# Row side of a gated linear attention: two-source copies of a, products, a guard and a copy on GpSimd, and stash copies in runs of four

## The chip, the cores and the metric

One NeuronCore of a Trainium2 chip runs the whole program. The metric is the device time of one execution, in microseconds (us). The engines are PE (TensorE, matrix products and transposes), DVE (VectorE), ACT (ScalarE), POOL (GpSimd), and SP (SyncE), whose queue issues most of the DMAs.

## The reference

Three layers follow one another. The first, which this change is about, is a linear attention whose state decays by a complex gate:

```python
scale = np.minimum(mag, 0.999) / (mag + 1e-06)      # mag = |a|
a_re_n, a_im_n = (a_re * scale, a_im * scale)
for t in range(S):                                  # S = 768
    new_re = ar * S_re - ai * S_im
    new_im = ar * S_im + ai * S_re
    S_re, S_im = (new_re + kv, new_im)              # kv: outer product of k and v
    y[:, :, t] = einsum('bhd,bhde->bhe', q[:, :, t], S_re)
```

Batch 4, 8 heads, head size 48. Behind it come a mixture of 8 experts on the tokens with a positive skip score, and a dense layer with a leaky activation (384 to 2048 to 384). All arrays are float32.

## The kernel before, in words

The batch is cut into two halves (`ui` 0 and 1), and the sequence into 8 chunks of 96 steps. A "row" is one chunk of one head of one sequence; a half has 128 rows, one per partition. Within a chunk the state is replaced by running products P of the gates: q is multiplied by P and k is divided by it, after which a chunk is matrix products. The row side (`attention_rows`, line 154) computes P, q times P and k over P for all 128 rows; the chunk side (`attention_chunks`, line 495) uses them. Both are done for half 0, then the experts and the dense layer of half 0 run woven with the row side of half 1, and so on.

The row side of half 0 works on blocks of steps (`BLKA`: one of 4 steps, ten of 8, then 6, 4 and 2). For each block there are these pieces:
- `load_a`, `load_kq` (lines 199, 205): DMAs on SP's queue. The tile of a has 3 buffers and that of k and q has 2, so `load_a(i + 3)` stands behind the last reader of block i's tile, in `norm` (line 251).
- `norm_pre` (211): on ACT squares, logarithm, exponential, square and the *guard* s2, a scale and an offset of r0. The sum of the two squares is a product with the identity on PE (tile `ad`, in PSUM), for blocks 0 to 2 a sum on DVE.
- `norm` (233): three steps on DVE into `nrr`, the third of which reads the guard; then the products of a with the scale, into columns 0 and 2 of the tile `a4`; then two copies into columns 3 and 1 of it, plain and negated (lines 255 to 261). Blocks 0 and 1 make these copies on DVE, others on ACT, and 11 to 13 the plain one on POOL (lists `MIRROR`, `MIRROR_G`; the guard of blocks 10, 11 and 13 is on POOL by `GUARD_G`).
- `steps` (335): the running product, one step after the other: a product of 192 elements into `t`, and a sum of 96 elements into P. The very first step is a copy of a into P (line 341).
- `scaled_pre`, `scaled` (263, 277): the norm of P on ACT and PE gives `pg`; on DVE two products of q with P (tile `qr`), two steps into `pu` (the first reads `ad` in PSUM and `pg`), a product into k, and two products of k with P (tile `kr`).
- `turned` (315): transposes on PE of four steps of `kr` or `qr` at a time into PSUM, and a copy by ACT into the *stash* (line 324), the layout the chunk side reads: partition = part and feature, then chunk, row and step.

In the same time `gate_products` (451) puts products of v with the gate weights on PE and ACT (tiles `gv`, `gvT`, `gps`).

Which instruction comes when is written by hand for half 0: `timed` (372) gives each piece a time in a plan (a block of n steps is 2n long, `AT_NORM`, `AT_SCALED` and so on are shares of it), and the instructions are issued in that order. DVE, ACT and PE keep it strictly (`keep("VAT")`); the order on POOL is left to the framework's scheduler, which takes what is ready, first what was written first. Every queue then runs in order. Before the row side is issued, the two stash tiles have their last 32 partitions zeroed on POOL:

```python
    gen = attention_rows(0, ep, BLKA, True, nc.sync, rws[0], stash, more)
    next(gen)
    constants()
...
    for x in stash:
        G.memset(x[2 * D:].rearrange("p c b t -> p (c b t)"), 0.0)
    run(gen)
```

The trace puts nearly all compute under line 91, the helper that records an instruction, so its rows are told apart by tile names.

Of the kernel before, what the change touches and what calls it, by code (L numbers as in the profile page):

```python
# [14 lines left out]
ALU = mybir.AluOpType  # L15
# [4 lines left out]
B, H, S, D = 4, 8, 768, 48  # L20
# [46 lines left out]
SUM_NORM = (0, 1, 2)  # L67
SUM_SCALED = (12, 13)
MIRROR = (0, 1)
GUARD_G = (10, 11, 13)  # L70
MIRROR_G = (11, 12, 13)
LISTS = dict(sp=(0, 1), tp=(2, 3, 7), yps=(4,), ups=(5,), tr=(6,), bk=(7,))
DEEP = {"kqt": 3, "vt": 3, "qT": 3}
LISTSA = dict(sp=(0, 1), yps=(2,), ups=(3,), tr=(4, 5, 6), bk=(7,))
# [4 lines left out]
def moe_attention_kernel(ctx, tc, q, k, v, a_re, a_im, w_skip, w_gate, w1, w2, w_in, w_out, out,  # L79
# [15 lines left out]
    V, A, T, G = Engine(nc.vector, "V"), Engine(nc.scalar, "A"), Engine(nc.tensor, "T"), Engine(nc.gpsimd, "G")  # L95
# [58 lines left out]
    def attention_rows(ui, ep, blks, sum_pe, queue, store, stash=None, more=None):  # L154
# [9 lines left out]
        nb = len(blks)  # L164
        tbm = max(blks)

        def rows(src, i):
            return src[b0:b0 + HB].rearrange("b h (c t) d -> c (b h) (t d)", t=L)[
                :, :, t0s[i] * D:(t0s[i] + blks[i]) * D]

        def flat(x):
            return x.rearrange("p t d -> p (t d)")

        def cost(i, n=1):
            return (70 + 1.04 * n * blks[i] * D) / 1e3

        def tl(tag, i, dims=(), after=(), bufs=None):
            kw = {} if bufs is None else {"bufs": bufs}
            t = ep.tile([R, *dims, tbm, *after, D], F32, tag=tag, name=tag, **kw)
            n = blks[i]  # L180
            return t[:, :, :n] if len(dims) == 1 else t[:, :n]

        def both(x, i):
            return x.unsqueeze(2).to_broadcast([R, blks[i], 2, D])

        a4s, Ps, ins, pre, turns, lags = {}, {}, {}, {}, [], []
# [12 lines left out]
        def load_a(i):  # L199
            ari = tl("ari", i, (2,), bufs=3)  # L200
            queue.dma_start(flat(ari[:, 0]), rows(a_re, i))
            queue.dma_start(flat(ari[:, 1]), rows(a_im, i))
            ins["a", i] = ari

        def load_kq(i):
            kq2 = tl("kq2", i, (2,))
            queue.dma_start(flat(kq2[:, 0]), rows(k, i))
            queue.dma_start(flat(kq2[:, 1]), rows(q, i))
            ins["k", i] = kq2

        def norm_pre(i):
# [14 lines left out]
            A.activation(rr, r0, AF.Square)  # L226
            if stash and i in GUARD_G:
                G.tensor_scalar(s2, r0, 0.5e-6 / MAGCAP, -0.5, ALU.mult, ALU.add)
# [4 lines left out]
        def norm(i):  # L233
            ari = ins.pop(("a", i))
            m2, s2, r0, rr = pre["a", i]
            V.tensor_tensor(rr, m2, rr, ALU.mult)
            yield cost(i)
            V.scalar_tensor_tensor(rr, rr, 3.0, r0, ALU.subtract, ALU.mult)
            yield cost(i)
            V.scalar_tensor_tensor(rr, rr, -2.0, s2, ALU.max, ALU.mult)  # L240
            yield cost(i)
            a4 = tl("a4", i, (), (4,))
            a4s[i] = a4
            if stash:
                V.tensor_tensor(a4[:, :, 0, :], ari[:, 0], rr, ALU.mult)
                yield cost(i)
                V.tensor_tensor(a4[:, :, 2, :], ari[:, 1], rr, ALU.mult)
            else:
                V.tensor_tensor(a4[:, :, 0::2, :], ari.rearrange("p c t d -> p t c d"), both(rr, i), ALU.mult)
            if i + 3 < nb:  # L250
                load_a(i + 3)
            yield cost(i, 2)
            for _ in range(3 if ui else 0):
                yield 0.0
            for c in range(2):
                if stash and i in MIRROR_G and not c:
                    G.tensor_scalar(a4[:, :, 3 - 2 * c, :], a4[:, :, 2 * c, :], 1.0 - 2 * c, None, ALU.mult)
                elif stash and i in MIRROR:
                    V.tensor_scalar(a4[:, :, 3 - 2 * c, :], a4[:, :, 2 * c, :], 1.0 - 2 * c, None, ALU.mult)
                else:  # L260
                    A.activation(a4[:, :, 3 - 2 * c, :], a4[:, :, 2 * c, :], AF.Copy, scale=1.0 - 2 * c)

        def scaled_pre(i):
            P = Ps[i]
            sq = ep.tile([R, tbm, 2, D], F32, tag="psq", name="psq")[:, :blks[i]]
            g0 = tl("pg0", i)
            A.activation(sq, P, AF.Square)
            yield
            n2 = added(sq[:, :, 0, :], sq[:, :, 1, :], i, SUM_SCALED)
            yield  # L270
            s2 = sq[:, :, 1, :]
            A.activation(s2, n2, AF.Ln)
            yield
            A.activation(g0, s2, AF.Exp, scale=-1.0)
            pre["k", i] = n2, g0

        def scaled(i):
            P = Ps.pop(i)
            kq2 = ins.pop(("k", i))
            u = tl("pu", i)  # L280
            if stash:
                kq = [tl(x, i, (), (2,)) for x in ("kr", "qr")]
            else:
                kq = tl("kq", i, (), (2, 2))
                kq = [kq[:, :, a] for a in range(2)] + [kq]
            if stash:
                V.tensor_tensor(kq[1][:, :, 0], kq2[:, 1], P[:, :, 0], ALU.mult)
                yield cost(i)
                V.tensor_tensor(kq[1][:, :, 1], kq2[:, 1], P[:, :, 1], ALU.mult)
            else:  # L290
                V.tensor_tensor(kq[1], both(kq2[:, 1], i), P, ALU.mult)
            yield cost(i, 2)
            n2, g0 = pre["k", i]
            V.tensor_tensor(u, n2, g0, ALU.mult)
            yield cost(i)
            V.scalar_tensor_tensor(u, u, 2.0, g0, ALU.subtract, ALU.mult)
            yield cost(i)
            V.scalar_tensor_tensor(kq2[:, 0], kq2[:, 0], -1.0, u, ALU.mult, ALU.mult)
            yield cost(i)
            if stash:  # L300
                V.tensor_tensor(kq[0][:, :, 0], kq2[:, 0], P[:, :, 0], ALU.mult)
                yield cost(i)
                V.tensor_tensor(kq[0][:, :, 1], kq2[:, 0], P[:, :, 1], ALU.mult)
            else:
                V.tensor_tensor(kq[0], both(kq2[:, 0], i), P, ALU.mult)
            if i + 2 < nb:
                load_kq(i + 2)
            if stash:
                turns.append(turned(i, kq))
            else:  # L310
                queue.dma_start(kqd[t0s[i]:t0s[i] + blks[i]].rearrange("t r a d -> r t (a d)"),
                                kq[2].rearrange("r t a c d -> r t (a c d)"))
            yield cost(i, 2)

        def turned(i, kq):

            for g in range(0, blks[i], 4):
                m = min(4, blks[i] - g)
                for a in range(2):
                    p = ps.tile([2 * D, m, R], F32, tag="qk", name="qkps")  # L320
                    for j in range(m):
                        T.transpose(p[:, j, :], kq[a][:, g + j].rearrange("p c d -> p (c d)"), ident)
                    t = t0s[i] + g
                    lags.append((stash[a][:2 * D, :, :, t:t + m].rearrange("p c b t -> p t (c b)"), p))
                    if len(lags) > 1:
                        A.activation(*lags.pop(0), AF.Copy)
                    yield
# [7 lines left out]
        def steps(i, prev):  # L335
            a4 = a4s.pop(i)
            P = ep.tile([R, tbm, 2, D], F32, tag="P", name="P", bufs=3)[:, :blks[i]]
            Ps[i] = P
            for t in range(blks[i]):
                if prev is None:  # L340
                    V.tensor_copy(P[:, t], a4[:, t, 0::2, :])
                else:
                    t4 = ep.tile([R, 2, 2, D], F32, tag="t4", name="t4", bufs=3)
                    V.tensor_tensor(t4, prev.unsqueeze(1).to_broadcast([R, 2, 2, D]),
                                    a4[:, t].rearrange("p (o i) d -> p o i d", i=2), ALU.mult)
                    yield 0.33
                    V.tensor_tensor(P[:, t], t4[:, :, 0, :], t4[:, :, 1, :], ALU.add)
                prev = P[:, t]
                yield 0.23
# [830 lines left out]
    stash = [p.tile([128, NCH, HB * H, L], F32, name="stash") for p in blocks]  # L1180
    ep = tc.alloc_tile_pool(name="rows0", bufs=2, side="right")
    more = []
# [3 lines that stand above are left out]
# [12 lines left out]
    rt = tc.alloc_tile_pool(name="rt", bufs=1, side="right")  # L1198
    ck[0].take(1)
    behind = attention_rows(1, ep, BLKB, False, nc.sync, rws[1])  # L1200

    def place(e, layer):
# [237 lines left out]
```

## Time and profile before

| | |
|---|---|
| median of 3 runs | 968.27 us (965.54 to 970.45) |
| the profiled execution's own time | 965.6 us |
| its span | 963.3 us |
| PE, DVE, ACT, POOL busy | 87%, 65%, 54%, 14% of the span |

The span runs from the first to the last instruction of the profiled execution; its own time is 2.3 us longer. Rows of the timeline give start, length, engine, line, operation, the written tile and what it reads, the shape, and in brackets the idle time before it with what ended it. "x2" is two instructions that follow each other, merged into one row. Instructions of an engine overlap a little, so the next can start before the last one's end.

### The profile page before, as it was taken

What the parts mean: (1) busy time and instruction counts of PE and PEld (TensorE: products, weight loads), DVE (VectorE), ACT (ScalarE), POOL (GpSimd) and SP (SyncE); (2) the same over time, 40 slices, a digit from 0 to 9 for tenths busy, and PEclk for the clock granted to TensorE, in tenths of its full rate; (3) what the DMA queues carried; (4) which work ended last, traced back from release to release, by engine and by line L of the source; (5) the groups of instructions that cost most, each with busy time, mean ns of one, the idle gap of its engine ahead of it and who ended that gap; (6) DMA issues with size and microseconds to landing.
All of it is one profiled execution on the core that took longest, in us unless ns stands there. A gap on an engine that the chain in (4) does not pass through costs nothing.

```text
span 963.3 us, 17827 instructions
## 1 busy us (share of the span) xinstructions
PE 835.0 (87%) x6674; PEld 581.0 (60%) x6674; DVE 628.5 (65%) x1534; ACT 517.9 (54%) x1065; POOL 137.2 (14%) x168
## 2 busy tenths in 40 slices
PE   0488877899569975699999988999999999999997
PEld 0366666899458853344556978945677645546454
DVE  7998796477868678999990456487668262260440
ACT  2578898566445443564751777656557162250430
POOL 9100011212163001100002211141101000000000
PEclk9978798999879988799999999999999999999999
DMA  4265552798848985625436799332857201000000
GB/s 113 70 184 149 149 143 87 201 264 268 272 152 280 318 289 181 222 86 177 145 97 174 196 256 246 107 119 100 266 182 246 79 9 51 17 0 26 9 10 27
DMA packets 126512, 143.61 MB, mean 149 GB/s; under 512 B 34058, under 2 KB 109514, under 8 KB 126416
## 3 DMA queue, kind: packets, MB, share of 16 engines
q1 hardware_dynamic: 106064, 107.88, 38.2%
q10 hardware_dynamic: 18304, 29.89, 9.6%
q0 software_dynamic: 2048, 4.61, 1.4%
q8 instruction: 54, 0.88, 0.4%
q14 instruction: 42, 0.34, 0.1%
HBM read 115.62 MB, written 28.41 MB: 150 GB/s over the span
## 4 chain that ended last, share of the span: by engine, by line
PE 52%; DVE 19%; DMA 15%; ACT 10%; issue 3%; SPq 1%; POOL 0%; ACTq 0%; DVEq 0%; POOLq 0%
PE ops L91 17%; PE hps L91 13%; PE yps L91 7%; PE sps L91 3%; DVE gg L91 3%; DMA raw<-in_moe_w_in_dram 3%; DVE gl L91 3%; DVE cst L91 3%; ACT stash L91 2%; DVE a L91 2%; ACT gh L91 2%; DMA kqt<-kqd 2%; PE tps L91 2%; PE ad L91 2%; DMA vt<-vd 2%
## 5 line engine op out<-in xcount | busy, mean ns | idle before, releaser
L91 PE MATMUL hps<-xTh,m2w 128*128 128x512 f16 x576 | 173.7, 381 | 0.4 <-ACT xTh L91 0.2
L91 PEld LDWEIGHTS <-m2w 128*128 128x128 f16 x864 | 84.4, 98 | 100.3 <-issue 3.2
L91 PE MATMUL ops<-m2w,gh 128*128 128x384 f16 x512 | 125.2, 326 | 0.0
L91 PE MATMUL hps<-xTl,m2w 128*128 128x512 f16 x288 | 109.3, 380 | 0.2 <-DVE xTl L91 0.2
L91 DVE TENSOR_TENSOR gg<-hps,gg 128x512 f32<-128x512 f32 x96 | 65.8, 686 | 65.1 <-ACT gg L91 64.7
L91 PE MATMUL ops<-m2w,gl 128*128 128x384 f16 x256 | 83.6, 327 | 0.0
L91 ACT ACTIVATE ot<-ops 128x384 f32<-128x384 f32 x24 | 11.6, 489 | 121.3 <-PE ops L91 121.3
L91 PEld LDWEIGHTS <-gh 128*128 128x128 f16 x512 | 50.1, 98 | 32.7
L91 DVE TENSOR_TENSOR t<-P,a 128x192 f32<-128x192 f32 x190 | 67.1, 353 | 1.3 <-ACT a L91 0.4
L91 PE MATMUL ops<-m2w,stash 128*128 128x384 f16 x384 | 65.3, 326 | 1.2 <-ACT m2w L91 1.2
L91 DVE TENSOR_TENSOR gl<-gg,gh 128x512 f16<-128x512 f32 x64 | 44.2, 690 | 33.9 <-ACT gh L91 33.2
L91 ACT ACTIVATE gg<-hps 128x512 f32<-128x512 f32 x96 | 56.3, 587 | 17.4 <-PE hps L91 12.0
L91 DVE SCALAR_TENSOR_TENSOR w<-cw,w 128x768 f16<-128x768 f32 x64 | 59.8, 953 | 7.3 <-ACT w L91 7.1
L91 ACT ACTIVATE gh<-gg 128x512 f16<-128x512 f32 x64 | 40.3, 630 | 42.9 <-DVE gg L91 42.7
L91 ACT ACTIVATE w<-cw 128x768 f16<-128x768 f32 x64 | 53.0, 843 | 18.1 <-DMA cw<-in_moe_w_dram 15.7
L91 POOL TENSOR_SCALAR_AFFINE_SELECT sc<-sc 96x384 f32<-96x384 f32 x64 | 35.2, 559 | 156.2 <-ACT sc L91 156.0
L91 PE MATMUL ad<-psq,ident 128*128 128x384 f32 (+2 forms) x48 | 24.9, 657 | 36.8 <-ACT psq L91 36.2
L91 PEld LDWEIGHTS <-stash 128*128 128x128 f16 x384 | 37.5, 98 | 28.6 <-issue 4.3
L91 POOL DMA_INDIRECT xd<-xo,idx x16 | 25.2, 1575 | 179.6 <-DVE xo L91 165.8
L91 ACT ACTIVATE stash<-qkps 96x512 f32<-96x512 f32 (+1 forms) x50 | 50.1, 1026 | 0.3 <-PE qkps L91 0.3
L91 DVE TENSOR_TENSOR P<-t 128x96 f32<-128x96 f32 x190 | 48.1, 253 | 1.6
L91 PE MATMUL yps<-stash,hh 128*128 128x384 f32 x128 | 44.7, 503 | 3.5 <-ACT hh L91 3.5
(245 smaller groups left out, 1786.1 us busy)
## 6 DMA issues: line engine op xcount, KB each, us to landing
stash<-in_moe_w_dram ACTq DMA_DIRECT2D x32, 768.0 KB
cw<-in_moe_w_dram SPq DMA_DIRECT2D x64, 384.0 KB
kqt<-kqd SPq DMA_DIRECT2D x16, 576.0 KB
kqd<-kq SPq DMA_DIRECT2D x14, 576.0 KB
vd<-gv SPq DMA_DIRECT2D x32, 192.0 KB
vt<-vd SPq DMA_DIRECT2D x32, 192.0 KB
raw<-in_moe_w_in_dram SPq DMA_DIRECT2D x16, 384.0 KB
raw<-in_moe_w_out_dram SPq DMA_DIRECT2D x16, 384.0 KB
```

The source lines that it names most:

```text
L91: ins = getattr(self.engine, op)(*args, **kw)
```

## The change

The plain copies of a that DVE makes in blocks 0 and 1 read the load and the scale again (two sources) in place of column 0 or 2 of `a4`, so the next load into that tile stands behind them. The first step of P is the maximum of a with itself. The guard of every block from 1 on, the plain copy of every block from 2 on and both products with q of blocks 0 to 10 are on POOL. The stash copy writes, for each feature, four steps in a row, and reads PSUM across the transposes.

```diff
-GUARD_G = (10, 11, 13)
-MIRROR_G = (11, 12, 13)
+GUARD_G = range(1, 14)
+MIRROR_G = range(2, 14)
+SCALED_G = range(11)
@@ norm
-            if i + 3 < nb:
+            if i + 3 < nb and not (stash and i in MIRROR):
                 load_a(i + 3)
...
                 elif stash and i in MIRROR:
-                    V.tensor_scalar(a4[:, :, 3 - 2 * c, :], a4[:, :, 2 * c, :], 1.0 - 2 * c, None, ALU.mult)
+                    V.scalar_tensor_tensor(a4[:, :, 3 - 2 * c, :], ari[:, c], 1.0 - 2 * c, rr, ALU.mult, ALU.mult)
                 else:
                     A.activation(a4[:, :, 3 - 2 * c, :], a4[:, :, 2 * c, :], AF.Copy, scale=1.0 - 2 * c)
+            if i + 3 < nb and stash and i in MIRROR:
+                load_a(i + 3)
@@ scaled
             if stash:
-                V.tensor_tensor(kq[1][:, :, 0], kq2[:, 1], P[:, :, 0], ALU.mult)
+                X = G if i in SCALED_G else V
+                X.tensor_tensor(kq[1][:, :, 0], kq2[:, 1], P[:, :, 0], ALU.mult)
                 yield cost(i)
-                V.tensor_tensor(kq[1][:, :, 1], kq2[:, 1], P[:, :, 1], ALU.mult)
+                X.tensor_tensor(kq[1][:, :, 1], kq2[:, 1], P[:, :, 1], ALU.mult)
@@ turned
-                    lags.append((stash[a][:2 * D, :, :, t:t + m].rearrange("p c b t -> p t (c b)"), p))
+                    lags.append((stash[a][:2 * D, :, :, t:t + m].rearrange("p c b t -> p (c b) t"),
+                                 p.rearrange("p t r -> p r t")))
@@ steps
-                    V.tensor_copy(P[:, t], a4[:, t, 0::2, :])
+                    V.tensor_tensor(P[:, t], a4[:, t, 0::2, :], a4[:, t, 0::2, :], ALU.max)
```

## Rows read from the trace of the kernel before

**Rows 1.** The page: busy time, share of the span and instructions of each engine.

```profile
PE 835.0 (87%) x6674; PEld 581.0 (60%) x6674; DVE 628.5 (65%) x1534; ACT 517.9 (54%) x1065; POOL 137.2 (14%) x168
```

**Rows 2.** Busy us by stretch: PE, PEld, DVE, ACT, POOL; clock, DMA share, GB/s.

```profile
60.00:70.00 10.00, 8.30 (x40) 5.95 (x40) 7.83 (x24) 6.84 (x14) 0.00 (x0) 0.66 0.63 161
...
120.00:130.00 10.00, 7.64 (x62) 6.01 (x61) 9.70 (x30) 9.62 (x20) 0.85 (x1) 1.00 0.57 146
...
146.00:164.00 18.00, 11.89 (x85) 9.14 (x84) 13.23 (x48) 17.10 (x37) 4.78 (x7) 0.87 0.29 86
```

**Rows 3.** Timeline of the start, 0 to 32 us, all engines.

```profile
0.96 0.15 POOL L91 MEMSET w<- 112x72 f32 x1
...
1.26 0.28 POOL masks.py:199 TENSOR_SCALAR_AFFINE_SELECT ident<-ident 128x128 f32<-128x128 f32 x1
...
6.35 20.73 POOL L91 MEMSET stash<- 32x12288 f32 x2
...
8.62 0.62 DVE L91 TENSOR_TENSOR a<-ari,nrr 128x192 f32<-128x192 f32 x2
...
9.16 18.04 DVE L91 TENSOR_SCALAR a<-a 128x192 f32<-128x192 f32 x2
...
10.28 0.51 ACT L91 ACTIVATE nsq<-nr 128x384 f32<-128x384 f32 x1
...
14.98 0.62 SPq L201 DMA_DIRECT2D ari<-in_a_re_dram  x1
...
28.56 0.55 DVE L91 SCALAR_TENSOR_TENSOR nrr<-nrr,nsq 128x384 f32<-128x384 f32 x1
...
30.75 0.60 SPq L201 DMA_DIRECT2D ari<-in_a_re_dram  x1
...
30.87 0.62 DVE L91 TENSOR_SCALAR a<-a 128x384 f32<-128x384 f32 x2
```

**Rows 4.** Timeline of DVE, 40 to 160 us: pu in five blocks, a q product.

```profile
47.35 0.55 DVE L91 TENSOR_TENSOR pu<-ad,pg 128x384 f32<-128x384 f32 x1
...
126.03 0.56 DVE L91 TENSOR_TENSOR pu<-ad,pg 128x384 f32<-128x384 f32 x1 [0.16 <-ACT pg L91]
...
135.94 0.56 DVE L91 TENSOR_TENSOR pu<-ad,pg 128x384 f32<-128x384 f32 x1 [0.48 <-ACT pg L91]
...
141.81 0.55 DVE L91 TENSOR_TENSOR qr<-kq,P 128x384 f32<-128x384 f32 x1
142.28 0.35 DVE L91 TENSOR_TENSOR t<-P,a 128x192 f32<-128x192 f32 x1
...
145.36 0.56 DVE L91 TENSOR_TENSOR pu<-ad,pg 128x384 f32<-128x384 f32 x1 [1.67 <-ACT pg L91]
...
152.71 0.46 DVE L91 TENSOR_TENSOR pu<-ad,pg 128x288 f32<-128x288 f32 x1 [1.21 <-ACT pg L91]
```

**Rows 5.** Waits, 36 to 165 us: who waited for whom, total, times, longest.

```profile
DVE pu L91 <- ACT pg L91: 13.7, 11, 2.8
```

**Rows 6.** Groups by shape, 0 to 180 us (the last: instructions of tile LG).

```profile
L91 ACT ACTIVATE stash<-qkps 96x512 f32<-96x512 f32 x46 | 48.0, 1063 | 0.0
...
L91 ACT ACTIVATE a<-a 128x384 f32<-128x384 f32 x18 | 8.4, 513 | 0.3 <-DVE a L91 0.2
...
L91 ACT ACTIVATE sT<-stp 96x512 f32<-96x512 f32 x2 | 1.2, 594 | 2.0 <-PE stp L91 1.9
...
L91 DVE TENSOR_REDUCE LG<-xps x32: 217/229/232, 177.8 to 629.1; 96x9 f32<-96x72 f32 x32
```

**Rows 7.** Timeline, 117 to 145 us: one-source operations of POOL, and a DVE product.

```profile
119.24 0.51 POOL L91 TENSOR_SCALAR nsq<-nr 128x384 f32<-128x384 f32 x1 [92.16 <-ACT nr L91]
...
132.16 1.25 POOL L91 TENSOR_SCALAR a<-a 128x288 f32<-128x288 f32 x1 [2.26 <-DVE a L91]
...
141.27 2.55 POOL L91 TENSOR_SCALAR a<-a 128x192 f32<-128x192 f32 x1 [7.86 <-DVE a L91]
...
132.53 0.58 DVE L91 TENSOR_TENSOR t<-P,a 128x192 f32<-128x192 f32 x1
```

## The prediction

> **What bounds it now.** I read the page first: over the whole span PE is the busiest engine [rows 1], but that is a mean, and the change touches one stage (but for one copy), the row side of the first half, which ends at 164 us. So the next view is the busy time by stretch. In 120 to 130 us DVE and ACT are both about 96% busy with PE's granted clock at 1.00; in 60 to 70 us PE is busy 8.30 of 10 us on two thirds of the matmuls at a clock of 0.66 (mostly its lower level, 1.2 GHz), and DVE idles; in 146 to 164 us ACT alone is full [rows 2]. All three take their instructions in a written order, so the one that is late holds the others.
>
> The timeline of the start shows the largest hole: DVE's two copies of a take 18.04 us, where such a tile's products ended in 0.62 us for two. They lie beside GpSimd's two memsets of the stash and end with them [rows 3]. During the same memset the two-source products on DVE ran at their usual length [rows 3]: a one-source copy is held by it, a two-source operation isn't.
>
> From there the pace is read at one DVE operation per block, the product into pu. From block 1 (47.35 us) to block 10 (145.36 us) are 9 periods, mean 98.01 / 9 = 10.89 us; the period from 126.03 to 135.94 us is 9.91 us, and there DVE hardly waits [rows 4]. The view of waits gives what the others lose: before pu DVE waited 11 times for ACT, 13.7 us [rows 5]. So ACT sets the long periods (directly, or by leaving PE idle, behind which its clock falls), and DVE the short ones.
>
> **Part 1, the two-source copies.** The block 0 copies and the first copy into P become two-source operations and, by the row of the products during the memset, aren't held: some 0.3 us each, done by 9.9 us. That would free 17 us. But the guard list now begins at block 1, and that guard is on GpSimd, whose queue has both memsets ahead of it: its input is there at 10.3 us, where ACT computed it before in 0.51 us, and the queue is free at 27.08 us [rows 3]. Behind it on DVE wait the third step of block 1's norm and, in order, everything else; ACT's next norm step waits for a sum of DVE there. With 0.51 us for the guard [rows 7] and 0.06 us for the release, that third step starts at 27.65 us instead of 28.56: 0.9 us gained, not 17. Block 1's two copies now run one element a cycle, 2 x 0.47 = 0.94 us instead of 0.62: 0.3 us back. **Start: -0.6 us.** The two loads of a that move behind the copies: block 3's comes to SP's queue after the loads of v anyway, at 14.98 us; block 4's (30.75 us) moves by about 0.3 us, with the next loads of v and k behind it on SP's queue. Its tile is wanted some 10 us later, so I cost it at nothing; without that cover it would be 0.3 us. The second half's row side also has the copy into P, once; a few hundredths of a us, under other work.
>
> The Trainium skill (SBUF — State Buffer, Who interferes with whom) says that a VectorE operation with two SBUF inputs contends with a GpSimd one that reads SBUF, not with one that only writes. The rows of the memset agree. It gives nothing for the in-order queue, on which my -0.6 us hangs.
>
> **Part 2, per block 2 to 10.** DVE loses two q products of 0.47 us each (0.55 long, the next starts 0.47 after) [rows 4]: -0.94 us. ACT loses a guard (0.51) and a copy (0.51 [rows 6]), in its overlapped stream 0.9 us together. GpSimd gets four operations that read SBUF. Its copy of 384 elements takes 0.51 us when alone; beside a dense DVE one of 192 elements took 2.55 us, and one of 288 elements 1.25 us while DVE's t went from 0.35 to 0.58 us [rows 7]. So they exclude each other, and DVE wins more often. What one costs in port time I take from the memset, 10.4 us / 12288 = 0.85 ns an element: 0.33 us for 384 (for 288 elements 0.24, near the 0.23 that t lost). A two-source product is not in the trace on GpSimd; bounds are 0.51 us (one source) and 2.55 us (starved); I take two passes, 0.65 us of port and 0.84 us in all, since nothing else differs from the nearest row, the 0.51. Sum per block: 2 x 0.33 + 2 x 0.65 = 1.96 us. DVE has two products per block with a PSUM operand (into nrr and pu), 2 x 0.47 = 0.94 us, under which GpSimd can read; 1.02 us remains. A DVE-bound block becomes 9.91 - 0.94 + 1.02 = **9.99 us**; with all of GpSimd's reads hidden 8.97, with none 10.93.
>
> The Trainium skill (GPSIMD Engine Reference, Engine selection) advises against two-input work on GpSimd, about twice as slow. From its 4497 ns for 2048 elements an estimate is 0.84 us for 384, and the sum would not change.
>
> Results come late but have room: a q product is wanted some 8 us after its issue, a guard or copy some 5 us. GpSimd has only these in its queue after 28 us.
>
> **Part 3, the stash copies.** Each writes 512 elements one stash row apart and takes 1063 ns; the copy of the same shape from PSUM that writes a dense row takes 594 [rows 6]. Runs of four should come near the latter. In exchange its PSUM source is read with a stride. DVE's reduction of 72 strided PSUM elements takes 229 ns [rows 6], about its fixed cost, so I expect no loss there; on ACT no row shows it. Bounds: 594 ns, or no better than 1063 (a loss isn't excluded). I take 594, -0.47 us each, 4 per block: with the 0.9 above ACT has 2.8 us less of about 9.5 per block. It is then no bound, PE has fewer idle spells, and the mean period should fall to DVE's: (10.89 - 9.99) x 9 = **-8.1 us** (bounds -17.3 and +0.4).
>
> From 146 to 164 us ACT is busy 17.10 of 18 us and DVE 13.23 [rows 2], waiting for ACT (1.21 us before block 11's pu [rows 4]). The dozen full copies there give back 12 x 0.47 = 5.6 us, DVE's idle 4.8 us is the most that can show; some of it is DVE's own dependences, so **-3 us** (bounds 0 and -4.8).
>
> **Sum.** 0.6 + 8.1 + 3 = 11.7 us; later stages begin that much sooner and are not touched. Against the profiled execution's own 965.6 us that is 953.9; it lies 2.7 us under the median of the three runs, so at the median 968.3 - 11.7 = **956.6 us**. Its own range is 945 to 966 by the bounds.
>
> **Rivals.**
> A, the start comes free. The order on GpSimd isn't always that of the code: the mask of ident ran at 1.26 us, behind a memset written later [rows 3]. If block 1's guard stands ahead of the memsets, or its wait is not as I read it, steps begin at about 11.3 instead of 27.65 us: 16.3 us more, 940.3. Against it: that swap was over a short wait, and both memsets are ready first.
>
> B, slower: GpSimd holds DVE out. Place: blocks 2 to 10. If each of its operations shuts DVE out for its full length (2 x 0.51 + 2 x 0.84 = 2.70 us, none of it under a product with a PSUM operand) and DVE waits 0.57 us for the guard besides, a block takes 9.91 - 0.94 + 2.70 + 0.57 = 12.24 us: +1.35 x 9 = 12.2, less 3.6 for start and tail, 976.9. It decides from a period of 10.89 us on. For it: the 2.55 us copy; against it: DVE's stretched t is the only one of that size. The Trainium skill (SBUF — State Buffer, Who interferes with whom) says that the second to issue blocks fully until the first ends. By that rule B is the outcome where GpSimd issues first; the trace has DVE winning mostly.
>
> C, the stash copies don't get faster, the strided PSUM read costing what the strided write did. Then ACT loses only 0.9 us a block, half of the middle's gain stays, none of the tail's: 0.6 + 4 = 4.6 us, 963.7.
>
> **Numbers.** My forecast 0.60, A 0.10, B 0.14, C 0.16. A measurement of this kernel tells a change from none at about 0.5%, 4.8 us. Faster: 0.55 of the forecast, A, and half of C, 0.72; same: 0.05, the rest of C and 0.04 of B, 0.18; slower: 0.10. From 940 to 969 lie the forecast, C and half of A; outside are some 0.17.
>
> **What would show it.** Right: GpSimd's first guard at 27 us with DVE waiting for it; copies into P before 10 us; stash copies near 0.6 us; pu to pu near 10 us with few waits for pg. Wrong: DVE running steps at 12 us (A); pu periods over 10.9 us, DVE's t well over 0.35 us, waits for GpSimd (B); stash copies at 1 us or more (C); DVE waiting for loads of a or kq, now wanted sooner.

## The result, and the profile after

The changed kernel runs in 961.05 us (median of 7 runs, 956.0 to 962.5) against 970.19 us before (median of 7): ratio 0.9914, 95% interval 0.9887 to 0.9942, or 8.3 us faster (5.6 to 11.0). The profiled execution took 961.61 us, with a span of 959.9. The forecast was 956.6 us, 11.7 us less than before. Four marks of the row side show where the time went; "first kps" is the chunk side's first transpose, which needs the whole stash.

| mark (start, us) | before | after | gained in the stretch |
|---|---|---|---|
| third norm step of block 1 | 28.56 | 27.56 | 1.00 |
| pu of block 1 | 47.35 | 48.35 | -2.00 |
| pu of block 10 | 145.36 | 141.61 | 4.75 |
| first kps | 164.11 | 157.27 | 3.09 |
| sum | | | 6.84 |

What follows the row side took 799.2 us of the one span and 802.6 of the other; over all the kernels below it took 798.4 to 806.3 us. So single profiles don't show the total to better than some 4 us, and the stretches are read instead.

The timeline of the start of the changed kernel (helper line 92 now):

```profile
6.32 20.61 POOL L92 MEMSET stash<- 32x12288 f32 x2
...
9.28 0.62 DVE L92 SCALAR_TENSOR_TENSOR a<-ari,nrr 128x192 f32<-128x192 f32 x2
9.81 0.25 DVE L92 TENSOR_TENSOR P<-a 128x96 f32<-128x96 f32 x1
...
27.02 0.51 POOL L92 TENSOR_SCALAR nsq<-nr 128x384 f32<-128x384 f32 x1
27.56 0.56 DVE L92 SCALAR_TENSOR_TENSOR nrr<-nrr,nsq 128x384 f32<-128x384 f32 x1 [15.62 <-POOL nsq L92]
```

The copies of a take 0.62 us beside the memset, where they took 18.04 [rows 3]: the two sources do what was said of them. Behind them and the first copy into P, DVE runs three more operations and stops. The bracket of the last row names the cause: 15.62 us for the guard on POOL, which starts when the memsets end.

Its groups by shape, 0 to 180 us, and one block in the timeline, DVE's rows first, then POOL's:

```profile
L92 DVE TENSOR_TENSOR t<-P,a 128x192 f32<-128x192 f32 x95 | 37.8, 397 | 0.8
L92 DVE TENSOR_TENSOR P<-t 128x96 f32<-128x96 f32 x95 | 29.0, 305 | 1.4
...
L92 ACT ACTIVATE stash<-qkps 96x512 f32<-96x512 f32 x46 | 26.5, 584 | 0.2
L92 POOL TENSOR_TENSOR qr<-kq,P 128x384 f32<-128x384 f32 x20 | 23.2, 1182 | 25.8 <-DVE P L92 23.4 <-PE gtps L92 2.5
...
L92 POOL TENSOR_SCALAR a<-a 128x384 f32<-128x384 f32 x9 | 13.7, 1522 | 21.3 <-DVE P L92 14.1 <-DVE a L92 7.2
```

```profile
101.39 0.55 DVE L92 TENSOR_TENSOR pu<-ad,pg 128x384 f32<-128x384 f32 x1
...
105.34 0.60 DVE L92 TENSOR_TENSOR P<-t 128x96 f32<-128x96 f32 x1
105.86 1.36 DVE L92 SCALAR_TENSOR_TENSOR nrr<-nrr,nr 128x384 f32<-128x384 f32 x1
...
109.08 0.55 DVE L92 TENSOR_TENSOR a<-ari,nrr 128x384 f32<-128x384 f32 x1
109.55 0.66 DVE L92 TENSOR_TENSOR t<-P,a 128x192 f32<-128x192 f32 x1
...
111.78 0.55 DVE L92 TENSOR_TENSOR pu<-ad,pg 128x384 f32<-128x384 f32 x1
...
104.46 2.35 POOL L92 TENSOR_TENSOR qr<-kq,P 128x384 f32<-128x384 f32 x2 [2.61 <-DVE P L92]
109.15 1.50 POOL L92 TENSOR_SCALAR a<-a 128x384 f32<-128x384 f32 x1 [2.35 <-DVE P L92]
111.64 0.59 POOL L92 TENSOR_SCALAR nsq<-nr 128x384 f32<-128x384 f32 x1 [0.99 <-POOL a L92]
```

The stash copy fell from 1063 to 584 ns. On DVE three rows of the block are too long, and each lies beside a POOL row: P 0.60 for 0.25 and nrr 1.36 for 0.55 beside the two q products (1.16 us in all), t 0.66 for 0.35 beside the copy of a (0.31 us). (The shorter lengths are those of the same rows in E3 below, where GpSimd has no work there.) The guard at 111.64 us falls under pu, whose operand is in PSUM, and costs nothing. The block takes 10.39 us, and DVE is busy without a gap. Its waits for ACT (27 to 165 us) are nearly gone, 1.5 for 13.7 us [rows 5], and the long one at the start stands in the same view:

```profile
DVE nrr L92 <- POOL nsq L92: 15.6, 1, 15.6
...
DVE pu L92 <- ACT pg L92: 1.5, 2, 1.0
```

### The profile page after: what moved, and what is told of

Same layout as the page of the kernel before. It is cut to its first block, busy times and chain, and to the rows that moved or that the text cites. A ratio compares the mean times of both kernels' runs of the same rounds, so it can differ in the third digit from the quotient of the medians.

```text
span 959.9 us, 17852 instructions
## 1 busy us (share of the span) xinstructions
PE 832.1 (87%) x6674; PEld 580.4 (60%) x6674; DVE 618.9 (64%) x1512; ACT 493.4 (51%) x1046; POOL 178.1 (19%) x209
## 4 chain that ended last, share of the span: by engine, by line
PE 53%; DVE 23%; DMA 12%; ACT 5%; issue 4%; POOL 2%; SPq 1%; ACTq 0%; DVEq 0%; POOLq 0%
PE ops L92 17%; PE hps L92 13%; PE yps L92 7%; PE sps L92 4%; DVE gg L92 3%; DMA raw<-in_moe_w_in_dram 3%; DVE t L92 2%; DVE cst L92 2%; DVE gl L92 2%; ACT gh L92 2%; PE tps L92 2%; PE ups L92 2%; DVE P L92 2%; DVE nrr L92 2%; DMA kqt<-kqd 2%
## 5 line engine op out<-in xcount | busy, mean ns | idle before, releaser
L92 DVE TENSOR_TENSOR t<-P,a 128x192 f32<-128x192 f32 x190 | 71.1, 374 | 1.6 <-ACT a L92 0.6
L92 DVE TENSOR_TENSOR P<-t 128x96 f32<-128x96 f32 x190 | 53.0, 279 | 1.9
L92 PE MATMUL ad<-psq,ident 128*128 128x384 f32 (+2 forms) x48 | 22.7, 609 | 33.6 <-ACT psq L92 33.5
L92 ACT ACTIVATE hh<-hps 128x256 f32<-128x256 f32 (+1 forms) x64 | 23.7, 377 | 41.1 <-PE hps L92 35.9
```

Of the source, the lines that this page charges most:

```text
L92: ins = getattr(self.engine, op)(*args, **kw)
```

## The experiments

Times are medians, ratios are to the kernel before, with their intervals. "Period" is the mean of the nine from block 1's pu to block 10's: 10.89 us before, 10.36 after.

**E1, block 1's guard back on ACT.**

```diff
-GUARD_G = range(1, 14)
+GUARD_G = range(2, 14)
```

> Block 1's guard back on ACT, all else as changed. Queue theory (the hole at the start is now block 1's guard behind the memsets in GpSimd's queue): DVE's third norm step of block 1 starts near 11.7 us instead of 27.56, and DVE stops about 7 us of work later, at block 2's third norm step, whose guard is now the first one behind the memsets, until 27.5 us. So about 7 us less than the changed kernel: 954 us. Rival (the first loads set the start): DVE waits for loads, not for GpSimd, and the time stays within 2 us of the changed kernel's.

954.7 us, ratio 0.9826 (0.9782 to 0.9870). The timeline:

```profile
27.02 0.51 POOL L92 TENSOR_SCALAR nsq<-nr 128x384 f32<-128x384 f32 x1
27.56 0.56 DVE L92 SCALAR_TENSOR_TENSOR nrr<-nrr,nsq 128x384 f32<-128x384 f32 x1 [9.82 <-POOL nsq L92]
```

The rows look like those of the changed kernel, but it is block 2's guard now, and the wait is 9.82 us for 15.62. Block 1's pu starts at 42.16 us, 6.19 earlier than in the changed kernel, near the 7 expected.

**E2, the guards of blocks 1 and 2 back on ACT.** The list is `range(3, 14)`.

> The guards of blocks 1 and 2 back on ACT. Queue theory: no DVE step before 27 us needs GpSimd any more (block 3's guard is wanted near 28 us), so steps run from 10 us on and the row side ends some 14 to 15 us sooner than in the changed kernel: 946 to 947 us. Rival (first loads): less than 5 us sooner.

950.3 us, ratio 0.9781 (0.9737 to 0.9825). Block 1's pu starts at 36.77 us, 11.58 earlier than in the changed kernel, not 14 to 15. The timeline says what is left:

```profile
27.02 1.19 POOL L92 TENSOR_SCALAR a<-a 128x384 f32<-128x384 f32 x1
...
28.25 0.74 DVE L92 TENSOR_TENSOR t<-P,a 128x192 f32<-128x192 f32 x1 [4.41 <-POOL a L92]
```

Next behind the memsets is block 2's plain copy of a, also new on POOL, for which the step t waits 4.41 us. I had forgotten it in the expectation; it is the same queue a third time.

**E3, the runs of four alone**, on the kernel before.

```diff
-lags.append((stash[a][:2 * D, :, :, t:t + m].rearrange("p c b t -> p t (c b)"), p))
+lags.append((stash[a][:2 * D, :, :, t:t + m].rearrange("p c b t -> p (c b) t"),
+             p.rearrange("p t r -> p r t")))
```

> The kernel before with only the stash copies in runs of four. Theory (these copies alone take ACT off the bound, and then DVE sets the period): stash copies 0.58 us, DVE's waits for pg nearly gone, pu to pu near 9.95 us (before 10.89, changed 10.36), the end of the row side 3 us less after block 10: about 11 us less than before, ratio 0.988. Rival (the operations moved to GpSimd were needed to unload ACT): periods stay over 10.4 us, less than 5 us gained.

952.88 us, ratio 0.9807 (0.9769 to 0.9846), 18.7 us faster than before (11 expected) and more than the whole change. The period is (133.53 - 47.32) / 9 = 9.58 us, and the first kps is at 149.0 us, 15.1 before that of the kernel before. Two blocks of the timeline's pu, the stretch ahead of it with the q products on DVE, and the waits:

```profile
66.54 0.55 DVE L91 TENSOR_TENSOR pu<-ad,pg 128x384 f32<-128x384 f32 x1
...
73.06 0.55 DVE L91 TENSOR_TENSOR a<-ari,nrr 128x384 f32<-128x384 f32 x1
...
76.15 0.55 DVE L91 TENSOR_TENSOR pu<-ad,pg 128x384 f32<-128x384 f32 x1
```

```profile
DVE pu L91 <- ACT pg L91: 1.7, 3, 1.0
```

With the lighter stash copies alone ACT no longer holds DVE, and a full block takes 9.61 us, less than the 9.91 that I had taken for DVE's own limit. The moves to GpSimd weren't needed for that. From the second product into a to pu there are 3.09 us with the q products; in the changed kernel 111.78 - 109.08 = 2.70, of which 0.31 is stretch. So taking two products from DVE saves 3.09 - 2.39 = 0.70 us, not 0.94: the steps left over wait for each other.

**E4, the two-source copies alone**, on the kernel before: the `norm` and `steps` parts of the diff, no list changed.

> The kernel before with only the two-source copies of a and the first step's copy. Queue theory: with no guard of an early block on GpSimd nothing on DVE waits for the memsets; steps begin near 10 us instead of 27, everything else unchanged: 17 us less than before, ratio 0.982. Rival (first loads): under 5 us gained, DVE or ACT waiting for DMAs between 10 and 27 us.

953.41 us, ratio 0.9828 (0.9780 to 0.9876), 16.7 us faster.

```profile
11.46 0.55 DVE L91 SCALAR_TENSOR_TENSOR nrr<-nrr,nsq 128x384 f32<-128x384 f32 x1
...
30.85 0.56 DVE L91 TENSOR_TENSOR pu<-ad,pg 128x384 f32<-128x384 f32 x1
```

The third norm step of block 1 starts at 11.46 us, 17.10 before that of the kernel before, with no wait, and block 1's pu 16.50 us earlier. ACT waits 2.65 us for a load of a, until 18.85 us, but no row of DVE waits behind it, so the rival falls.

**E5, runs of four and two-source copies together**, no new work on GpSimd.

> The kernel before with the two-source copies and the runs of four, without any of the new GpSimd work. Theory (start hole 17 us, middle and tail 11 us, independent of each other): 28 us less than before, ratio 0.971, pu to pu near 9.95 us. Rival (with both gone the loads, wanted 17 us sooner and at a faster pace, become late): under 22 us gained, with DVE or ACT waiting for DMAs of a, k or q.

934.58 us, ratio 0.9667 (0.9634 to 0.9701): 32.3 us faster than before, and faster than both kernels of this case. The gain expected was 28 us. The two rows of pu give a period of 9.45 us:

```profile
31.32 0.56 DVE L91 TENSOR_TENSOR pu<-ad,pg 128x384 f32<-128x384 f32 x1 [0.25 <-ACT pg L91]
...
116.40 0.54 DVE L91 TENSOR_TENSOR pu<-ad,pg 128x384 f32<-128x384 f32 x1
```

The sum of E3's and E4's gains is 35.4 us, so the two are nearly independent, as expected. ACT waits 2.36 us for one load of a, until 18.91 us, and no row of DVE waits behind it: late loads play no part. The first kps is at 131.8 us.

**E6, the q products back on DVE** in the changed kernel, `SCALED_G = ()`.

> The changed kernel with the q products back on DVE. Theory (two products cost DVE 1.16 us of stretch per block on GpSimd and 0.94 us on DVE itself): pu to pu 10.36 - 0.22 = 10.14 us, so 2 us less in the middle than the changed kernel, and its start hole unchanged: ratio to the changed kernel 0.998, that is 959 us. Rival (the move to GpSimd relieves DVE): periods near 10.9 us and 5 us slower than the changed kernel.

954.15 us, ratio 0.9857 (0.9827 to 0.9887), where 959 was expected, and a period of 9.86 us. The products on GpSimd cost 10.36 - 9.86 = 0.50 us a block, twice what I expected. By the rows it is 1.16 lost and 0.70 saved, 0.46; in the expectation I still had 0.94 saved.

**E7, the old stash copies** in the changed kernel.

> The changed kernel with the old stash copies (one element at a time). Theory (with guard and copy off ACT it is busy some 8.6 us a block, below DVE's 10.36): the middle loses little, pu to pu 10.4 to 10.6 us, and the tail loses its 3 us: 3 to 5 us slower than the changed kernel, 964 to 966 us. Rival (the runs carry the middle): periods back at 10.9 us or more, 8 us or more slower, no faster than the kernel before.

962.7 us, ratio 0.9927 (0.9905 to 0.9948), a period of 10.50 us. Its interval overlaps that of the changed kernel, so the total alone doesn't tell them apart; its first kps is at 161.6 us, 4.3 later. With guard and plain copy off ACT, and DVE slowed by GpSimd, the runs bring little in the middle, and DVE hardly waits for ACT there. The rival falls. Its period's two ends, and the waits:

```profile
48.38 0.55 DVE L92 TENSOR_TENSOR pu<-ad,pg 128x384 f32<-128x384 f32 x1
...
142.92 0.55 DVE L92 TENSOR_TENSOR pu<-ad,pg 128x384 f32<-128x384 f32 x1
```

```profile
DVE pu L92 <- ACT pg L92: 2.1, 4, 1.1
```

The kernel before has 10.89 us and 13.7 us of these waits. So without the runs the moves to GpSimd do take ACT off the bound (the two-source copies lie ahead of this stretch): they alone bring 0.39 us a block, where the runs alone (E3) bring 1.31.

**E8 and E9, the GpSimd work in two parts**, each on E5, from blocks where no memset is in the way.

```diff
 # E8
+SCALED_G = range(2, 11)         # the q products, as in the change
 # E9
-GUARD_G = (10, 11, 13)
-MIRROR_G = (11, 12, 13)
+GUARD_G = range(3, 14)
+MIRROR_G = range(3, 14)
```

> The kernel with only runs of four and two-source copies, plus the q products of blocks 2 to 10 on GpSimd. Port theory: DVE gets rid of 2 products but its own steps then wait for each other, net 0.70 us a block, and loses 1.16 us of stretch: pu to pu from 9.45 up by 0.46 to 9.9 us, 4 us slower than without, 941 us. Rival (the price seen in the changed kernel came from the four operations queueing together): periods at or below 9.45 us, no slower.

941.65 us, ratio 0.9733 (0.9671 to 0.9796), a period of 10.22 us: 0.76 over E5. The first of the nine took 12.04 us, with waits for ACT in it (31 to 45 us); the eight behind it average 9.99, 0.58 over the same eight of E5 (9.41).

> The same base, with guard and plain copy of blocks 3 on on GpSimd and the q products on DVE. Port theory: only the copy stretches DVE (0.31 us a block), ACT was not the bound any more: periods 9.45 to 9.75 us, 2 to 3 us slower than without, 939 to 940 us. Rival (ACT's relief still helps): at or below 9.45 us.

938.83 us, ratio 0.9694 (0.9643 to 0.9745), a period of 9.83 us: 0.38 over E5. By the totals neither E8 nor E9 is told from E5 (the intervals overlap), by the periods both are: each is from one execution, but E5's 9.45 us came again as 9.44 in E10 below. The DVE rows between 31 and 117 us of E8 (first two) and of E9 show where:

```profile
L92 DVE TENSOR_TENSOR P<-t 128x96 f32<-128x96 f32 x66 | 20.2, 307 | 1.1
...
L92 DVE SCALAR_TENSOR_TENSOR nrr<-nrr,nr 128x384 f32<-128x384 f32 x7 | 6.2, 892 | 0.0
```

```profile
L91 DVE TENSOR_TENSOR t<-P,a 128x192 f32<-128x192 f32 x69 | 27.6, 400 | 0.3
```

The products stretch P (0.25) and norm steps (0.55), the copy stretches t (0.35). Neither part pays on E5.

**E10 and E11, what GpSimd's work costs DVE.** On E5, one more operation on GpSimd per block, whose output nobody reads: a memset, or a copy of P.

```diff
+                if i in range(2, 11):
+                    scr = ep.tile([R, 8, 2, D], F32, tag="scr", name="scr", bufs=1)
+                    G.tensor_scalar(scr[:, 0, 0, 0:1], P[:, 0, 0, 0:1], 1.0, None, ALU.mult)
+                    G.memset(scr, 0.0)                                   # E10
+                    G.tensor_scalar(scr, P, 1.0, None, ALU.mult)         # E11
```

> The same base, plus extra GpSimd work that only writes SBUF: a memset of 768 elements per block 2 to 10 (after a read of one element), some 0.73 us. Port theory (a GpSimd operation costs DVE by what it reads): DVE's t and P keep 0.35 and 0.25 us, periods stay at 9.45 us. Rival (any GpSimd work holds DVE): t or P stretched by 0.4 to 0.7 us once a block.

> The same, with a copy of the 768 elements of P in place of the memset: it reads and writes. Port theory: 0.85 ns an element is 0.65 us of port, so a t or P (or another two-source operation) is stretched by about that once a block and periods rise to 9.9 to 10.1 us, less what falls under a product with a PSUM operand. Rival: as the memset, no stretch.

One execution each: 934.83 and 935.93 us. The groups between 31 and 117 us, of E10 and then of E11:

```profile
L91 DVE TENSOR_TENSOR P<-t 128x96 f32<-128x96 f32 x72 | 18.1, 252 | 0.9
...
L91 DVE SCALAR_TENSOR_TENSOR nrr<-nrr,nr 128x384 f32<-128x384 f32 x7 | 3.8, 548 | 0.0
...
L91 POOL MEMSET scr<- 128x768 f32 x8 | 5.9, 738 | 0.5
```

```profile
L91 DVE TENSOR_TENSOR P<-t 128x96 f32<-128x96 f32 x68 | 18.5, 272 | 0.9
...
L91 DVE SCALAR_TENSOR_TENSOR nrr<-nrr,nr 128x384 f32<-128x384 f32 x7 | 4.4, 635 | 0.0
...
L91 POOL TENSOR_SCALAR scr<-P 128x768 f32<-128x768 f32 x9 | 22.5, 2504 | 48.6 <-DVE P L91 48.5
```

The memset takes 0.74 us (0.73 expected), and DVE's rows are as in E5; the period is 9.44 us. The copy of as many elements takes 2.5 us, and DVE's P and nrr grow; the period is 9.84 us. So it is the reading that collides. My size was too high (9.9 to 10.1 us expected): of the 0.39 us over E5 the stretched rows hold some 0.3, where I had expected 0.45 to 0.65. The copy lies beside the product into nrr with an operand in PSUM, which may have covered part of it; that was not tested. The rest is waits for ACT, 1.2 us over the stretch.

## Why the prediction was right, point by point

- **Direction and size.** 8.3 us measured (5.6 to 11.0), 11.7 forecast, which is above the interval. The mechanisms were those it named, but by the marks the sum was 4.9 us too high, 1.6 of it ahead of block 1's pu and 3.4 in the middle. In the middle two values were off in opposite directions; that the forecast came so near is in part luck.
- **The start.** The forecast was that the 18 us hole stays, because block 1's guard is put behind the memsets, and that the third norm step starts at 27.65 us. It started at 27.56. E1, E2 and E4 show that cause: each operation taken out of GpSimd's queue moves the hole to the next one, and with none there it goes. Rival A, to which I gave 0.10, did not happen.
- **Blocks 0 and 1.** The sum has only the two-source copies of block 1 there, 0.3 us (1.02 for 0.62 measured, so 0.4); it counts GpSimd's price from block 2 on. Their GpSimd operations cost DVE as much: between 27.56 and 48.35 us eight DVE rows beside them are longer by 2.7 us in all, the nrr below by 0.80. Four q products less on DVE give back part of that, and 2.00 us are lost, those of the table. So up to block 1's pu 1.0 us was lost where 0.6 was to be gained: that step failed by omission.

```profile
41.08 2.29 POOL L92 TENSOR_TENSOR qr<-kq,P 128x384 f32<-128x384 f32 x2 [2.13 <-DVE P L92]
...
42.44 1.35 DVE L92 SCALAR_TENSOR_TENSOR nrr<-nrr,nr 128x384 f32<-128x384 f32 x1
```

- **The middle** is the mis-sized term, -8.1 us forecast and -4.75 measured. Two values in it were wrong. DVE's own limit for a full block was not 9.91 us but 9.61 (E3). The period that I took ends with a wait for ACT of 0.48 us and holds a t of 0.58 beside a GpSimd copy; and it was not a full block, as its norm is block 11's, of 288 elements. In E3 the same period takes 9.33 us. And the GpSimd work: I took 0.94 us saved and 1.02 lost; measured are 0.70 saved and 0.31 + 1.16 = 1.47 lost. 9.61 - 0.70 + 1.47 = 10.38 us, and the timeline has 10.39. The price of an operation was near (0.33 us for the copy, 0.65 for a q product; 0.31 and 0.58 measured); what failed is the overlap. Of 1.96 us I put 0.94 under products with a PSUM operand, and only 0.49 did not show. The two-source product takes 1.18 us on GpSimd (0.84 assumed).
- **PE's clock.** The prediction let ACT act also through it. Between the two pu of the table the mean granted clock was 0.86 before, 0.91 after, 0.94 in E3 and 1.00 in E5. In E7 the waits for ACT went from 13.7 to 2.1 us at 0.88, so the lower clock alone did not make them; its share is not separated here.
- **The stash copies.** 584 ns, 594 forecast: rival C falls. E3 shows that they alone would gain (10.89 - 9.58) x 9 = 11.8 us in the middle, two and a half times the 4.75 of the whole change. In the changed kernel they bring little there: without them (E7) the middle gains 3.5 us. Either way of relieving ACT makes DVE the bound, so the two don't add, and the moves then set DVE a slower pace. The prediction added them.
- **The end of the row side.** -3 forecast, -3.09 measured.
- **Rival B** was the right kind of cost. GpSimd's reads hold DVE, though by a part of their length. The Trainium skill (SBUF — State Buffer, Who interferes with whom) has the reads contend and the writes not; E10 and E11 agree (no stretch beside a 738 ns memset, P 272 for 252 and nrr 635 for 548 ns beside the copy). It also has the second to issue blocked fully; here both are held in part: DVE for 0.31 us of a copy that took 1.52.
- **The load moved behind the copies** went from 30.75 to 30.96 us (0.3 forecast; DVE was 1.0 us earlier there), and nothing waited for it.
- **Two slips in the prediction's sums.** The chances as listed give 0.73 faster and 0.17 same, not 0.72 and 0.18; and the bounds, added at the median, end at 968 us and not at 966. The measured time lies inside either.

So the two-source copies could bring 17 us and are kept from it by the guard's place in GpSimd's queue. The runs of four could bring as much, and the moves to GpSimd, which help ACT where the old stash copies hold it (E7), cost time beside the runs: E5, without the moves, gains 32.3 us.

## What to carry to other kernels

When work moves to an engine that looks idle, read its queue in order of time first: what stands ahead there is inherited by whoever waits. An operation on GpSimd that reads SBUF isn't free for VectorE, so a product moved there pays only if VectorE has the time to lose; and which engine is the bound can change with another part of the same change. And measure each part alone; here the runs and the two-source copies without the moves give four times the gain of all.

## What the runs showed of the hardware that I had not expected

- ACT reads PSUM with a stride of 128 elements at no loss: 584 ns for 96 x 512 elements, against 594 for the dense read of the same shape [rows 6]; it was the write, one stash row apart, that cost the 1063.
- Beside a dense DVE, a one-source copy of 768 elements on GpSimd took 2504 ns and cost DVE some 0.3 us, but a two-source product of 384 elements took 1182 ns and cost DVE 0.58 us. Who is held longer depends on the kind; why was not tried.
